# Attention in two half sweeps, then a feed-forward block: scores and exponentials of the first ten steps made one step ahead, in areas of five PSUM banks

## Chip, cores and metric

The kernel runs on one core of a Trainium2 chip. The metric is device time in microseconds of one execution, lower is better. Engines: TensorE (PE) for matmuls, VectorE (DVE), ScalarE (ACT), GpSimd (POOL) and SyncE (SP), which issues most DMAs.

## What is computed

```python
# q, k, v: (8, 8, 576, 64) fp32; tau = 0.02
scores = scale * np.matmul(q, k.transpose(0, 1, 3, 2))       # scale = 1/8
thresh = np.max(scores, axis=-1, keepdims=True) - tau
scores = np.where(scores >= thresh, scores, -1000000000.0)
scores = scores - np.max(scores, axis=-1, keepdims=True)
attn = np.exp(scores)
attn = attn / (np.sum(attn, axis=-1, keepdims=True) + 1e-09)
x = np.matmul(attn, v)              # then (B,H,S,D) -> (B*S, H*D) = (4608, 512)
h = x @ w_in                        # w_in (512, 2048)
g = np.maximum(h, 0.0) ** 2
out = g @ w_out                     # w_out (2048, 512)
```

## The kernel before

Attention runs over "visits". A visit is one pair of heads of one batch; within it a "step" is one block of 128 queries (blocks 0 to 3, and a last block of 64, index 4, which is handled for both heads together). The first batch is done in two sweeps over its four head pairs (`visits`, L813): visits 0 to 3 take query blocks 0 and 1 (steps 0 to 7), visits 4 to 7 take blocks 2, 3 and 4 (steps 8 to 19). In this way the first 256 output rows of all heads are ready after step 10, and the feed-forward work on them (`chunk_at`, L851, pieces placed by `fill`, L929) starts there. Steps before that are called early (`early()`, L863). Later visits take all five blocks in one go. All engines' orders are written out by hand: the loop at L1096 emits instructions, and each engine runs its own in that order.

A step consists of:

- `scores` (L258): per head two matmuls over 288 keys each into PSUM, then `maxima` (L304), one reduce on DVE per head. Scores of a step go to `pairs[0:2]`, banks 0 to 3, of step 1 to banks 4 to 7. The matmul of one head uses the upper 64 rows of the array, of the other the lower 64.
- `exponents` (L319): on ACT a scaled maximum (L322), a threshold (L323) and one exponential per head (L325) from PSUM to one of three slots for weights.
- `threshold` (L328): on DVE, per head, one operation that compares the scores in PSUM with the threshold, multiplies and sums (L337), then a small reduce and a reciprocal. `divide` (L342): on POOL one small and two large operations (L345, L347).
- two steps later `turn` (L378): nine 128x128 transposes on PE in three parts, each part into a bank from `take`, and copied to `wT` by ACT (L387).
- three steps later `mix` (L499): twenty records of value matmuls on PE (L502) into a bank from `take("tx", (4, 5))`, copied to `xT` by ACT (L485).

Around it: `load_qk` (L171) loads queries and keys of a visit, all 576 rows of both, as 32-column pieces, by DMAs that SP issues; `prep` (L232) turns them on DVE (L247) into `qT` (one buffer) and `kT` (two buffers). A piece of the feed-forward weights is rounded in some steps (`pieces`, L935; `round_weights`, L138): two operations on ACT (L149, L150), two on DVE (L152, L154), two on POOL (L156, L158), and a new piece is then loaded (L136, 512 KB). In the early steps that is the first step of visits 1, 2 and 3, and every step from 8 on.

The order of an early step s before, from the loop at L1096: scores of s, parts 0 and 1 of the turn of s-2, exponents of s, values of s-3, part 2 of the turn of s-2, threshold of s, rounding, divide. In the last step of a visit the next visit's queries and keys are turned (`lay`, L1126). The parts of a turn take banks 4, 5 and, for part 1, 6, 7.

`AT` (L113) is a table of four areas of 576 columns that the last part of the kernel uses, two per head, alternating between odd and even blocks; neighbours share a bank:

```python
AT = {(0, 0): (128, 384), (0, 1): (704, 320), (1, 1): (1280, 256), (1, 0): (1856, 192)}
```

The first number is where an area begins in PSUM (512 columns make a bank), the second how many of its columns lie before the next bank.

## Time and profile before

| | us |
|---|---|
| median of three runs | 1335.18 (1333.57 to 1335.2) |
| profiled execution | 1333.83 |
| its span | 1332.0 |
| PE busy in the span | 1295.4 (97%) |
| DVE, ACT, POOL busy | 927.9, 583.0, 786.0 |
| 30 to 60 us: PE, DVE, ACT, POOL busy | 25.65, 24.41, 21.85, 17.59 of 30 |
| 60 to 140 us: PE, DVE, ACT, POOL busy | 73.31, 60.35, 60.04, 68.88 of 80 |

How to read it: busy times are sums over one execution on the core; the ends of matmuls are modelled, so a busy PE is not PE at its peak. A row of a timeline or of a chain has the start in us from the span's start, the length, the engine, the line of the code and how many records were merged (a matmul in fp32 is two records). In brackets stands how long the engine was idle before, and the instruction that ended it.

### The profile page before, as it was taken

The page shows a single profiled execution, that of the slowest core. Times are in us where ns is not written, and L with a number is a line of the kernel's source. Part 1 is how long each engine was busy: PE and PEld are TensorE (multiplying, and loading weights), DVE is VectorE, ACT ScalarE, POOL GpSimd, SP SyncE. Part 2 cuts the span into 40 slices and gives each one's busy share as a digit, 9 for nine tenths or more (in the row PEclk, how much of TensorE's full clock was granted, in tenths as well). Part 3 has the DMA queues.
Part 4 walks back from the last instruction along what each step waited for, and adds up shares of the span by engine and source line. Part 5 has one row for each costly group of instructions (what it writes and reads, how often), then busy time and mean ns, then how long its engine had stood idle before and what let it go on. Part 6 is the DMA issues. An engine that isn't in the chain of part 4 may idle for free.

```text
span 1332.0 us, 25215 instructions
## 1 busy us (share of the span) xinstructions
PE 1295.4 (97%) x9112; PEld 1078.0 (81%) x9112; DVE 927.9 (70%) x2026; ACT 583.0 (44%) x1357; POOL 786.0 (59%) x915
## 2 busy tenths in 40 slices
PE   7898899999999999999999999999999999999998
PEld 5676556888787979797878878888897988889997
DVE  6877776877777878787777776868687877632131
ACT  4776674235262625343534343434443443421321
POOL 4689875775755565474665665747474747454351
PEclk7999999999999999999999999999999999999999
DMA  8764531648786968776766776676686767520000
GB/s 159 160 153 117 144 91 36 159 111 184 166 196 140 214 152 199 167 172 161 167 155 157 163 179 166 168 149 172 148 186 143 178 150 161 161 70 6 12 17 16
DMA packets 330126, 186.69 MB, mean 140 GB/s; under 512 B 291441, under 2 KB 291473, under 8 KB 323601
## 3 DMA queue, kind: packets, MB, share of 16 engines
q1 hardware_dynamic: 317696, 116.87, 46.5%
q0 software_dynamic: 10000, 67.92, 12.8%
q8 instruction: 72, 1.18, 0.4%
q10 hardware_dynamic: 2304, 0.29, 0.2%
q14 instruction: 54, 0.43, 0.1%
HBM read 109.22 MB, written 68.42 MB: 133 GB/s over the span
## 4 chain that ended last, share of the span: by engine, by line
PE 86%; DVE 4%; ACT 3%; POOL 2%; DMA 2%; issue 1%; SPq 0%; ACTq 0%; DVEq 0%; POOLq 0%
PE big L659 29%; PE big L765 28%; PE big L502 10%; PE big L289 8%; PE big L548 3%; PE big L273 3%; PE big L730 2%; PE big L386 2%; DVE st L310 1%; ACT wT L387 1%; DMA wT<-aside 1%; DVE w L337 1%; ACT w L325 1%; DMA aside<-turned 1%; POOL w L347 1%
## 5 line engine op out<-in xcount | busy, mean ns | idle before, releaser
L337 DVE SCALAR_TENSOR_TENSOR w<-big,st,w 128x576 f32<-128x576 f32 x269 | 207.1, 805 | 96.8 <-ACT w L325 96.5
L310 DVE TENSOR_REDUCE st<-big 128x1 f32<-128x576 f32 x288 | 204.2, 748 | 93.8 <-PE big L289 61.7
L347 POOL TENSOR_SCALAR w<-w,st 128x576 f32<-128x576 f32 x269 | 246.6, 926 | 26.4 <-DVE st L340 21.4
L765 PE MATMUL big<-wo,gsum 128*128 128x256 f32 x1088 | 243.8, 382 | 0.0
L765 PEld LDWEIGHTS big<-wo,gsum 128*128 128x128 f32 x1088 | 204.4, 190 | 37.0 <-issue 8.1
L659 PE MATMUL big<-xT,w_in_sb 128*128 128x128 f32 x1536 | 187.4, 277 | 1.3 <-DVE g L671 1.2
L659 PEld LDWEIGHTS big<-xT,w_in_sb 128*128 128x128 f32 x1536 | 178.5, 192 | 10.6 <-issue 8.1
L765 PE MATMUL big<-wo,g 128*128 128x256 f32 x816 | 185.3, 382 | 0.1
L325 ACT ACTIVATE w<-big,st 128x576 f32<-128x576 f32 x269 | 183.8, 734 | 0.0
L765 PEld LDWEIGHTS big<-wo,g 128*128 128x128 f32 x816 | 151.6, 190 | 26.1 <-issue 6.5
L502 PE MATMUL big<-wT,vs 128*64 128x128 f32 (+5 forms) x1700 | 164.2, 355 | 8.3 <-ACT wT L387 4.2
L502 PEld LDWEIGHTS big<-wT,vs 128*64 128x64 f32 (+1 forms) x1700 | 97.1, 137 | 72.0 <-issue 20.7
L322 ACT ACTIVATE st<-st 128x2 f32<-128x2 f32 (+1 forms) x148 | 30.3, 205 | 258.2 <-DVE st L310 257.1
L345 POOL TENSOR_SCALAR st<-st 128x2 f32<-128x2 f32 (+1 forms) x148 | 35.2, 238 | 169.3 <-DVE w L337 163.5
L408 POOL DMA_DIRECT2D aside<-turned x50 | 29.9, 597 | 177.9 <-DVE turned L437 173.7
L671 DVE TENSOR_TENSOR g<-big,g 128x512 f32<-128x512 f32 x96 | 64.7, 676 | 82.4 <-PE big L659 76.8
L289 PE MATMUL big<-kT,qT 64*128 64x256 f32 (+3 forms) x768 | 106.9, 416 | 0.0
L289 PEld LDWEIGHTS big<-kT,qT 64*128 64x128 f32 x768 | 84.5, 186 | 14.5 <-issue 5.0
L667 ACT ACTIVATE g<-g 128x512 f32<-128x512 f32 x96 | 60.2, 628 | 62.9 <-DVE g L671 62.7
L538 POOL TENSOR_TENSOR gsum<-g 128x512 f32<-128x512 f32 x34 | 46.2, 1358 | 69.8 <-ACT g L668 69.6
L668 ACT ACTIVATE g<-g 128x512 f32<-128x512 f32 x128 | 80.7, 630 | 4.1
L431 DVE STREAM_TRANSPOSE turned<-w 128x512 f32<-128x512 f32 x100 | 70.2, 702 | 0.0
(114 smaller groups left out, 2039.0 us busy)
## 6 DMA issues: line engine op xcount, KB each, us to landing
aside<-turned POOLq DMA_DIRECT2D x50, 1152.0 KB, 4.8
wT<-aside SPq DMA_DIRECT2D x200, 288.0 KB, 5.4
vs<-in_v_dram SPq DMA_DIRECT2D x72, 128.0 KB, 6.1
ql<-in_q_dram SPq DMA_DIRECT2D x126, 72.0 KB, 5.0
wo<-in_moe_w_in_dram SPq DMA_DIRECT2D x16, 512.0 KB, 4.6
wo<-in_moe_w_out_dram SPq DMA_DIRECT2D x16, 512.0 KB, 3.8
out_dram<-osb POOLq DMA_DIRECT2D x32, 256.0 KB, 3.6
kl<-in_k_dram SPq DMA_DIRECT2D x113, 72.0 KB, 2.9
```

The source lines that it names most:

```text
L289: nc.tensor.matmul(big[to, at + x0:at + x1], lhsT, keys[u * D:(u + 1) * D, x0:x1], start=True, stop=True)
L310: nc.vector.tensor_reduce(out=mx[:, u:u + 1], in_=sc[u], axis=AX.XY, op=ALU.max)
L325: nc.scalar.activation(out=w[:, u, :].rearrange("p (h k) -> p h k", h=2), in_=sc[u], func=AF.Exp, bias=bias[:, u:u + 1], scale=SCALE)
L337: nc.vector.scalar_tensor_tensor(out=wu, in0=sc[u], scalar=thr[:, u:u + 1], in1=wu, op0=ALU.is_ge, op1=ALU.mult, accum_out=sm[:, u:u + 1])
L347: nc.gpsimd.tensor_scalar(out=w[:, u, :], in0=w[:, u, :], scalar1=z[:, u:u + 1], scalar2=rcp[:, u:u + 1], op0=ALU.add, op1=ALU.mult)
L431: move(wb[:, 0:h, :, :], whole_[:, 0, :, :, :])
L502: nc.tensor.matmul(ps[u * D:(u + 1) * D, :], vs[n % 2][rows, u * (NBLK + 1) + c, :], wT[rows, at // REST:(at + ps.shape[1]) // REST, NBLK ...
L659: nc.tensor.matmul(to[:, f, :], factor(j, p, q, c)[:, f * P:(f + 1) * P], part[:, c, :], start=(p in "125" and f == 0 and c == 0), stop=(p ...
L667: nc.scalar.activation(out=to, in_=to if src is None else src, func=AF.Relu)
L668: nc.scalar.activation(out=to, in_=to, func=AF.Square)
L671: nc.vector.tensor_tensor(out=x, in0=to, in1=x, op=ALU.add)
L765: nc.tensor.matmul(to, left[:, f, :], wo[:, slot, f, :], start=(f == 0), stop=(f == HF - 1))
```

## The change

Seven edits, all in the first 20 steps. First, early steps get a function of their own, `early_step`: scores and exponents of step s+1 are emitted in step s, before the threshold of s. Second, for steps 2 to 9 the scores go to the four areas of `AT`, by turns for odd and even steps, in banks 0 to 4, and each head's matmuls are cut at the bank's edge. Third, turns and values of early steps take their banks from 5, 6, 7, and the three copies of a turn come behind the exponents on ACT. Fourth, in the early steps the next visit's queries and keys are turned in the first step of a visit, not in the last. Fifth, in the two sweeps of the first batch only the queries of the sweep's own blocks are loaded and turned (8 or 10 of 18 blocks of 32 rows), and the keys of the first visit are turned in two halves. Sixth, the weight pieces of visits 1 to 3 are rounded in their second step. Seventh, the small operation on `ntau` goes from DVE to POOL. From step 10 on the instructions follow each other as before, but for the narrower loads and turns of the queries of visits 5 to 7.

```diff
+    def columns(t, n):
+        first = FIRST * P // 32
+        return slice(0, S // 32) if t is k or n >= 2 * HP else slice(0, first) if n < HP else slice(first, S // 32)
...
     def load_qk(n):
         for x, t in ((rows_of(n)[1], k), (rows_of(n)[0], q)):
+            cols = columns(t, n)
             for m in range(4):
...
-                queue.dma_start(out=to[:, last:, :], in_=src[:, 0:S // 32 - last, :])
+                queue.dma_start(out=to[:, cols.start + last:cols.stop, :], in_=src[:, cols.start:cols.stop - last, :])
...
     def prep_part(t, n):
-        nc.vector.transpose(to, rows.rearrange("p c d -> p (c d)"))
+        for x in (slice(0, HALF // 32), slice(HALF // 32, S // 32)) if t is k and n == 0 else (columns(t, n),):
+            nc.vector.transpose(to[:, x.start * 32:x.stop * 32], rows[:, x, :].rearrange("p c d -> p (c d)"))
...
     def scores(s):
-        if i == NBLK:
+        if 1 < s < min(chunk_at):
+            for u in range(n):
+                at, cut = sorted(AT.values())[2 * u + s % 2]
+                rows = slice(u * D, (u + 1) * D)
+                for x0, x1 in ((0, cut), (cut, S)):
+                    nc.tensor.matmul(big[:, at + x0:at + x1], qT[rows, i * P:(i + 1) * P], kT[vis % 2][rows, x0:x1],
+                                     start=True, stop=True)
+                sc[u] = big[:, at:at + S].rearrange("p (h k) -> p h k", h=2)
+        elif i == NBLK:
...
     def turn(vis, i, part):
-        ps = take("mm", (6, 7)) if early() and part == 1 else take("tx", (4, 5))
+        ps = take("tx", (5, 6, 7) if early() else (4, 5))
...
-            nc.scalar.copy(wT[:, 2 * i:2 * i + 2, 3 * part:3 * part + 3, :].rearrange("p g c q -> p c g q"),
-                           ps[:, 0:3, :].rearrange("p c (g q) -> p c g q", g=2))
+            return lambda: nc.scalar.copy(wT[:, 2 * i:2 * i + 2, 3 * part:3 * part + 3, :].rearrange("p g c q -> p c g q"),
+                                          ps[:, 0:3, :].rearrange("p c (g q) -> p c g q", g=2))
...
     def mix(n, cols):
-            ps = take("tx", (4, 5))[:, 0:cols.stop - cols.start]
+            ps = take("tx", (5, 6, 7) if early() else (4, 5))[:, 0:cols.stop - cols.start]
...
-            x = int(n > 0 and i == 0)
+            x = int(n > 0 and i == 1)
...
-    nc.vector.tensor_scalar(out=ntau8, in0=ntau8, scalar1=-1.0 / SCALE, scalar2=None, op0=ALU.mult)
+    nc.gpsimd.tensor_scalar(out=ntau8, in0=ntau8, scalar1=-1.0 / SCALE, scalar2=None, op0=ALU.mult)
...
+    def early_step(s):
+        n, i = steps[s]
+        first = i == visits[n][1][0]
+        now = list(range(sum(pieces[:s]), sum(pieces[:s + 1])))
+        if first and n + 2 < 2 * HP:
+            load_qk(n + 2)
+        if s == 0:
+            scores(0)
+            exponents(*steps[0])
+        if s + 1 < min(chunk_at):
+            scores(s + 1)
+        if first and n < HP:
+            prep(n + 1)
+        if not first:
+            split_left(n)
+        copies = [turn(*steps[s - 2], part) for part in range(3)] if s > 1 else []
+        if s + 1 < min(chunk_at):
+            exponents(*steps[s + 1])
+        for fn in copies:
+            fn()
+        for p in now:
+            round_weights(p, 0)
+        if s in mixes:
+            mix(*mixes[s])
+        threshold(n, i)
+        for p in now:
+            for stage in (1, 2, 3):
+                round_weights(p, stage)
+        divide(n, i)
+        for p in now:
+            end_rounding(p)
+        if first and n:
+            load_v(n)
...
     for s in range(END + 1):
         state["step"] = s
+        if early():
+            rounded_by.append(state["rounded"])
+            done += pieces[s]
+            early_step(s)
+            continue
```

## Prediction

> **What bounds the kernel now.** I read first the page's busy slices, then the chain of work that ended last in the first 100 us, then single instructions of that stretch. The slices: over the span TensorE (PE) is nearly full, except in the first two slices (33 us each). There a saving or a loss moves the end; the change touches only this stretch and the loads of steps 10 to 19.

> ```profile
> PE   7898899999999999999999999999999999999998
> PEclk7999999999999999999999999999999999999999
> ```

> The chain in order of time (start, us, engine and line), here step 8's scores to step 9's:

> ```profile
> 49.19 1.97 PE big L273 x7
> 51.16 0.49 PE big L386 x3
> 51.65 0.02 issue
> 51.67 0.86 ACT wT L387 x2
> 52.53 0.10 ACT st L322
> 52.64 0.05 ACT st L323
> 52.69 0.04 issue
> 52.73 0.75 ACT w L325
> 53.48 0.02 issue
> 53.51 0.84 DVE w L337 x2
> 54.34 0.04 issue
> 54.39 1.97 PE big L273 x7
> ```

> A closed loop: scores, a turn, two copies, the first exponential, the threshold, and then the next scores, which overwrite the banks that the threshold read. It is 5.20 us, and scores stand 5.20 apart at 33.60, 38.80, 43.99, 49.19 and 54.39; steps 2 and 3 took 6.85 and 7.26 (scores at 14.70, 21.55, 28.81). No engine is full in it. The links that the new order needs, from the timeline (start, length, engine, line; in brackets idle time and who ended it):

> ```profile
> 28.81 1.56 PE L273 MATMUL big<-kT,qT 64*128 64x288 f32 x8
> 50.46 1.49 DVE L310 TENSOR_REDUCE st<-big 128x1 f32<-128x576 f32 x2 [0.20 <-PE big L273]
> 57.93 1.37 ACT L325 ACTIVATE w<-big,st 128x576 f32<-128x576 f32 x2
> 59.19 0.49 ACT L242 COPY qmid<-qT 64x64 f32<-64x64 f32 x2
> 65.99 0.86 ACT L387 COPY wT<-big 128x384 f32<-128x384 f32 x2 [0.48 <-PE big L386]
> 66.52 1.31 PE L502 MATMUL big<-wT,vs 128*64 128x128 f32 x20 [0.24 <-ACT wT L387]
> 67.76 0.55 PE L386 MATMUL big<-ident,w 128*128 128x128 f32 x3
> ```

> The reader sees: maxima start 50.46 - 49.19 = 1.27 after their scores start (the wait was for PE) and last 1.49; two exponentials hold ACT for 59.19 - 57.93 = 1.26; the values' matmuls start 66.52 - 65.99 = 0.53 after the copy that they wait for, and hold PE for 67.76 - 66.52 = 1.24.

> [...] the L386 x3 at 67.76 start only as the values end. [...] PE idled 3.82 us before 14.70, the granted clock was 0.50 from 16 to 28, eight score records took 3.02 us there and 1.56 at 28.81.

> **The change part by part.**

> *The new loop.* In steps 2 to 9 the order on PE is: scores of s+1, nine transposes of s-2, values of s-3. On ACT: exponents of s+1, three copies of s-2, rounding, the copy of the values. A step takes four banks out of three (5, 6, 7), so the values of s-3 write the bank that the first copy of s-2 must have read. That is an added wait: the values wait for a copy, which stands behind the exponents of s+1 on ACT, which wait for maxima, which wait for scores. Behind the values on PE stand the scores of s+2, and the maxima wait for them. So one step cannot be shorter than: scores to maxima 1.27; two maxima to ACT's first small operation 1.46 + 0.03 (pipelined, 1.45 to 1.49 in the rows); small operations to first exponential 0.31 (52.42 to 52.73); exponentials 1.26; first copy to values 0.53; values 1.24. Sum 6.10, against 5.20: +0.90 a step. The threshold has left the loop; maxima, the second exponential and the values have entered. I take 6.10; bounds 5.7 (scores of both heads overlap, as the 1.56 hints) and 6.5 (the second exponential also overwrites the slot that the transposes of s-2 read: those end at scores start + 1.6 + 1.4 + 0.2 = 3.2, while it starts at 3.07 + 0.64 = 3.71, so it costs nothing unless they slip by 0.5). Bank waits of the thresholds on the exponents of s+1 end at exponents' start + 3.0; the next scores start at + 3.03: covered, barely.

> *Engines' own floor.* DVE per two steps: four maxima 2.98, four thresholds 3.18 (53.51 to 55.10 is two), small ones 0.56, rounding 0.85, transposes 0.36 + 0.73: 8.67, 4.33 a step. ACT: 2 x (0.31 + 1.26 + 3 x 0.37 + 0.17) + 1.25 = 6.95, 3.5 a step. Neither binds.

> *Start.* Scores 0 stood at 8.57, behind two transposes (7.08 to 8.52) and DVE's ntau. Now q has 8 of 18 blocks, k is turned in halves, ntau goes to POOL (idle then; its DMA landed before, and ACT needs it only after 10): gone, but the twenty warm-up transposes hold PE to 7.76, so scores 0 at 7.8, -0.8. Scores 2 then at 13.9 (same 6.13 behind), cold clock, 3.02; maxima end 17.7, first exponential to 18.7; scores 3 (whose parts share banks with those of step 2, so wait for its exponentials) 18.7 to 21.9; nine transposes at half clock 2.2 (17.66 to 19.84), to 24.1; the threshold of step 2 starts behind the exponential of step 3, scores 4 at about 24.9, against 28.81. But step 3 then still runs at half clock: 6.10, + 0.96 for one head's scores, + about 0.4 of the values: scores 5 at 32.4 against 33.60, -1.2. Bounds -2.2 (clock back at 25) and +0.5 (back after 33).

> *Steps 5 to 8:* four intervals, 4 x 0.90 = +3.6.

> *The hand-over.* Step 10 keeps the old order, so its scores are not made ahead: from scores 9, the values of step 5 end at 6.10, transposes of step 7 to 7.5; ACT finishes three copies (5.5), rounding 1.25 (6.75), the values' copy and qmid (7.2), then the copy that the values of step 6 wait for: 7.73, + 1.24 = 8.97, scores 10. Before, 59.73 - 54.39 = 5.34: +3.6.

> *Smaller edits, at nothing.* q's smaller loads are as many DMAs, and SP's issue is 0.49 each for 8 KB or 72 KB; no engine waited for a DMA from 28 to 60. They save DMA packets only. Narrower transposes save 0.4 of DVE a visit, beside DVE's wait for the exponential (0.2 to 1.1 a step). The transposes move one step earlier, past a threshold: q of visit 3, issued by 26.1, landed 2.7 later and was read at 36.28, so 7.5 of slack less a 6.1 step remains 1.4; if that cover fails, 1 us once. A weight piece (ACT 1.25, DVE 0.85, POOL 2.5, one 512 KB DMA on SP) goes from first to second steps; five are done by step 9 both ways, and POOL's 4.4 in such a step lies within 6.1. From step 10 the programs agree, so the delay is carried: PE is busy 73.3 of 80 us from 60 to 140 and 1176 of 1192 after.

> Sum: -1.2 + 3.6 + 3.6 = +6.0. The profiled execution took 1333.83 (span 1332.0, 1.83 around it): 1339.8. The median of the runs shown is 1335.18, 1.35 above that execution; on it 1341.2, said as 1341.0.

> **The rivals.**

> *Faster, 0.07.* The values' wait for the first copy costs less than I think (the copy ends before PE gets there), and DVE becomes the bound at 4.33 to 4.6. The profile's idle DVE speaks for it, the closed chain of waits against. It decides where the step falls below about 4.9, since 5 steps and 2.7 of hand-over behind 32.4 must then reach scores 10 before 59.73. At 4.5 the loop gives 32.4 + 22.5 + 2.7 = 57.6, -2.1, and with a good start and a shorter hand-over -4: 1331.

> *No difference, 0.13.* Step 5.4: 5 x 0.7 less and the better start (-2.2): +1.5, 1336.7. For it: concurrent heads in the scores, start of step 4 four us earlier. Against: the maxima are DVE's 1.46 whatever PE does.

> *Clock stays low, 0.12.* PE would be busy about 4.0 of 6.1 us (before: 4.0 of 5.2), with a gap of 1.5. If the clock drops or comes back late, each cold step adds 0.96 + 1.1; three to four such steps give 7 on top of the 6.0: 1348. Against: such a step is 80% busy, which restored the clock at 28.

> **The numbers.** Forecast 0.68 at 1341.0, its own range 1338 to 1345. Range for all: 1336.5 (no difference) to 1347 (late clock). This kernel's measurement tells about 0.2%, 2.7 us, from no change. Faster 0.07, same 0.13, slower 0.80.

> **What would show it.** Right: the first values row of each step waits for a copy of ACT; scores 6.1 apart from step 5; maxima wait for scores; about 9 us from scores 9 to 10; DVE and ACT idle more from 30 to 60. Wrong: spacing under 5, DVE without idle time, the clock at 0.5 past 33, or a delay at step 10 that has shrunk by 140 us.

## The result, and the profile after

The change made the kernel slower: 1343.84 us (median of 4 runs, 1341.88 to 1344.95) against 1334.46 (4 runs), a ratio of 1.0069, 95% interval 1.0056 to 1.0082. The profiled execution has a span of 1341.1 us against 1332.0, so +9.1; 6.0 had been worked out. By the medians it is +9.4.

The busy slices of the page after the change. The first two are lower than before (33.5 us each); of the rest only the fifth differs, 9 for 8:

```profile
PE   6698999999999999999999999999999999999998
PEclk7899999999999999999999999999999999999999
```

PE is less busy in both (6 and 6 tenths, before 7 and 8), and its clock is lower in the second (8 tenths, before 9). What the slices can't show is where. The start of each step's scores on PE's timeline does:

| scores of step | 0 | 2 | 3 | 4 | 5 | 6 | 7 | 8 | 9 | 10 | 11 |
|---|---|---|---|---|---|---|---|---|---|---|---|
| before | 8.57 | 14.70 | 21.55 | 28.81 | 33.60 | 38.80 | 43.99 | 49.19 | 54.39 | 59.73 | 64.23 |
| after | 7.69 | 14.06 | 18.13 | 24.07 | 31.74 | 38.27 | 45.40 | 51.92 | 59.05 | 68.53 | 73.68 |

The changed program leads by 4.7 us at step 4 and by 1.9 at step 5, is 4.7 behind at step 9, 8.8 at step 10 and 9.5 at step 11. A scores group that stood at 210.36 before stands at 219.90: the delay is carried to the end.

The chain of the changed kernel in order of time (start, length, engine, tile and line), for the step that answers to the one shown of before:

```profile
37.03 1.31 PE big L517 x20
38.34 1.18 PE big L276 x6
...
39.54 1.44 DVE st L325 x2
...
41.00 0.03 ACT st L337
...
41.29 1.35 ACT w L340 x2
42.64 0.38 ACT wT L402
...
43.07 2.40 PE big L517 x20
45.47 1.65 PE big L276 x6
```

This is the loop that the prediction drew: values (L517), scores, two maxima, the small operations, two exponentials, the first copy, and the values again. The threshold has gone from it. From 37.03 to 43.07 it took 6.04. But the next values are the same twenty records, and take 2.40 instead of 1.31: they run at half clock.

PE's timeline after (in brackets: idle time, and who ended it):

```profile
43.07 2.40 PE L517 MATMUL big<-wT,vs 128*64 128x128 f32 x20 [2.42 <-ACT wT L402]
...
50.68 1.31 PE L517 MATMUL big<-wT,vs 128*64 128x128 f32 x20 [2.43 <-ACT wT L402]
...
56.72 2.40 PE L517 MATMUL big<-wT,vs 128*64 128x128 f32 x20 [2.42 <-ACT wT L402]
```

From 37.03 on every step's values wait for the copy, with PE idle 2.42 to 2.43 us, and every second step is then cold (its values run at half clock). The values' starts lie 6.04 and 7.61 apart by turns, 13.65 for two.

Stretches of the changed kernel show when the clock falls (columns: stretch, its length, busy us of PE, PEld, DVE, ACT and POOL, granted clock, DMA share, GB/s):

```profile
36.18:39.59 3.41, 2.56 (x29) 2.12 (x30) 1.76 (x7) 1.82 (x5) 1.90 (x4) 1.00 0.43 73
39.59:43.01 3.42, 1.06 (x9) 0.82 (x8) 1.71 (x3) 2.01 (x6) 0.20 (x1) 1.00 0.30 68
43.01:46.42 3.41, 3.35 (x25) 3.02 (x27) 2.30 (x8) 2.17 (x6) 0.85 (x1) 0.50 0.12 17
46.42:49.83 3.41, 1.83 (x14) 1.24 (x12) 2.67 (x5) 1.22 (x4) 3.24 (x5) 1.00 1.02 225
```

The stretches are laid so that the clock is the same within each: in the first 100 us of this trace it changes only at borders that lie 3.41 us or a multiple of it apart (low from 15.70 to 22.53, 25.94 to 32.77, 43.01 to 46.42 and 56.66 to 60.08). In the one ahead of the fall at 43.01 PE was busy 1.06 of 3.42 us (31%). The stretch at 0.50, busy 3.35 of 3.41, is followed by 1.00 again; the stretch with 1.83 (54%) is followed by one more at 1.00. The busy share is not all that counts, as the parts on half of the array's rows and on the clock below show. In the trace of before the clock was low from 14.77 to 28.42, which is 13.65, or four times 3.41. In the changed kernel's trace two steps last 13.65 us, as long as the four stretches above (36.18 to 49.83), so the same step of each pair meets the emptiest stretch, and the falls at 43.01 and 56.66 lie 13.65 apart.

### The profile page after: what moved, and what is told of

Read it like the earlier page. It is cut to its first block, busy times and chain, and to the rows that moved or that the text cites. A ratio compares the mean times of both kernels' runs of the same rounds, so it can differ in the third digit from the quotient of the medians.

```text
span 1341.1 us, 25225 instructions
## 1 busy us (share of the span) xinstructions
PE 1294.9 (97%) x9112; PEld 1078.6 (80%) x9112; DVE 928.6 (69%) x2026; ACT 583.4 (44%) x1357; POOL 787.8 (59%) x916
## 3 DMA queue, kind: packets, MB, share of 16 engines
q8 instruction: 72, 1.18, 0.4%
## 4 chain that ended last, share of the span: by engine, by line
PE 86%; DVE 4%; ACT 3%; POOL 3%; DMA 2%; issue 1%; SPq 0%; DVEq 0%; POOLq 0%; ACTq 0%
PE big L674 28%; PE big L780 28%; PE big L517 11%; PE big L304 8%; PE big L563 3%; PE big L745 2%; PE big L288 2%; DVE st L325 2%; PE big L401 2%; ACT w L340 1%; PE big L276 1%; DMA wT<-aside 1%; DVE w L352 1%; ACT wT L402 1%; POOL w L362 1%
## 5 line engine op out<-in xcount | busy, mean ns | idle before, releaser
L325 DVE TENSOR_REDUCE st<-big 128x1 f32<-128x576 f32 x288 | 204.2, 748 | 102.0 <-PE big L304 60.6
L517 PE MATMUL big<-wT,vs 128*64 128x128 f32 (+5 forms) x1700 | 166.0, 358 | 21.2 <-ACT wT L402 17.2
L780 PEld LDWEIGHTS big<-wo,g 128*128 128x128 f32 x816 | 151.6, 190 | 26.1 <-issue 6.5
L517 PEld LDWEIGHTS big<-wT,vs 128*64 128x64 f32 (+1 forms) x1700 | 98.7, 139 | 85.2 <-ACT wT L402 22.1
L337 ACT ACTIVATE st<-st 128x2 f32<-128x2 f32 (+1 forms) x148 | 30.2, 204 | 279.7 <-DVE st L325 278.7
```

The lines of the kernel that those rows point to most:

```text
L325: nc.vector.tensor_reduce(out=mx[:, u:u + 1], in_=sc[u], axis=AX.XY, op=ALU.max)
L517: nc.tensor.matmul(ps[u * D:(u + 1) * D, :], vs[n % 2][rows, u * (NBLK + 1) + c, :], wT[rows, at // REST:(at + ps.shape[1]) // REST, NBLK ...
L780: nc.tensor.matmul(to, left[:, f, :], wo[:, slot, f, :], start=(f == 0), stop=(f == HF - 1))
```

## The experiments

Each ratio is to runs of the kernel before that were made on the same chip together with the kernel compared (medians 1333.53, 1333.69 and 1333.53; for the changed kernel it was 1334.46). A loss is therefore given against those runs of before. Where a kernel has one added line above, its line numbers are one higher than the changed kernel's.

**The first copy ahead of the exponents.** It takes the values' wait out of the loop with the order alone.

```diff
         copies = [turn(*steps[s - 2], part) for part in range(3)] if s > 1 else []
+        for fn in copies[:1]:
+            fn()
         if s + 1 < min(chunk_at):
             exponents(*steps[s + 1])
-        for fn in copies:
+        for fn in copies[1:]:
             fn()
```

> The changed kernel, with the first of the three copies of a turn put ahead of the exponents of s+1 on ACT, so that the values no longer wait behind the exponents; nothing else moves. Loop theory (values wait for that copy, and scores of s+2 stand behind the values on PE): the wait goes, the next limit is DVE and the banks shared with the exponents, steps 5.4 to 5.5 us apart where the changed kernel has 6.0 at full clock and 6.8 on average; four intervals give 5 to 6 us, and the hand-over at step 10 stays at about 9: 1337.5 to 1339.5. Clock theory alone (the loop is 6.0 anyway and only the low clock costs): scores stay 6.0 or more apart, 1340 or more. Order theory (what costs is that DVE has the maxima of s+1 ahead of the threshold of s): no change, 1343 to 1344.

Measured 1335.95 (21 runs), ratio 1.0017 (1.0010 to 1.0023): moving one copy takes the loss from 9.4 to 2.4 us. The time lies below the range of the loop theory: the steps are shorter than it had them (5.29 for 5.4 to 5.5), the hand-over is longer, and the runs of before made with it are 0.9 lower. The two other theories had 1340 or more, and fell. Scores from step 5 on stand at 30.45, 35.60, 41.03, 46.19 and 51.62, 5.29 apart on the mean. PE's timeline of this kernel:

```profile
38.64 1.31 PE L517 MATMUL big<-wT,vs 128*64 128x128 f32 x20
41.03 1.97 PE L276 MATMUL big<-kT,qT 64*128 64x320 f32 x8 [1.08 <-DVE w L352]
```

The values no longer wait, and the wait that is left is that of the scores for a threshold: that of two steps back, since odd and even steps take the areas by turns and these scores overwrite the area that it read. The clock stays at 1.00 from 30 to 59. Of the 7.05 us won at scores 10 (61.48 against 68.53), 1.29 are there at scores 5, 6.14 are won from there to scores 9, and 0.38 are lost in the hand-over, 9.86 here: PE waits there for POOL and ACT, one stretch (56.42 to 59.83) is 52% busy, and the clock falls at 59.83.

**Something for PE to do in the gap.** It leaves the loop as it is and fills part of PE's wait with six 128x128 matmuls of `ident`, whose output nobody reads.

```diff
+    FILL = 6
...
         copies = [turn(*steps[s - 2], part) for part in range(3)] if s > 1 else []
+        if copies and s + 1 < min(chunk_at):
+            free = bank[(5, 6, 7)[used["tx"] % 3]][:, 3 * P:4 * P]
+            for _ in range(FILL):
+                nc.tensor.matmul(free, ident, ident, start=True, stop=True)
```

> The changed kernel with six more matmuls of 128 columns (1.3 us) behind the transposes of each of steps 2 to 8, into unused columns, in the 2.4 us in which PE waits for the copy. Clock theory (the gap lets the clock fall in every second step, which then takes 1.6 us more): clock 1.00 from 30 to 60, steps 6.0 to 6.1 apart, four intervals give 3, the hand-over 0.5: 1340 to 1341. If the clock's falls have nothing to do with the gap: 0.5 stays in every second step, time as in the changed kernel or up to 1 more. If the low clock did not cost anything: clock 1.00, time unchanged.

Measured 1338.44 (5 runs), ratio 1.0036 (1.0023 to 1.0048): more work for PE, and the loss falls from 9.4 to 4.9 us. Its timeline, and then its stretch from 30 to 60 us:

```profile
39.05 1.50 PE L1133 MATMUL big<-ident 128*128 128x128 f32 x12
41.63 1.31 PE L518 MATMUL big<-wT,vs 128*64 128x128 f32 x20 [1.08 <-ACT wT L403]
```

```profile
30.00:60.00 30.00, 24.62 (x245) 21.18 (x243) 21.32 (x51) 18.17 (x47) 16.05 (x21) 1.00 0.52 112
```

The clock is 1.00 throughout (0.84 without the filling), and scores from step 5 on (30.79, 36.83, 42.87, 48.91, 54.95) are 6.04 apart each time. From step 5 on this is the loop by itself, with no clock in it; what stays of the loss, 4.9 us, is the loop and the hand-over (8.99), less the earlier start. It came out lower than expected, in part because the clock was up in step 4 too (scores 5 at 30.79), in part because the runs of before made with it are 0.9 lower.

**Three instead of six** (`FILL = 3`).

> The run with the filling matmuls, but three in place of six, so that a gap of about 1.8 us stays on PE in each of steps 2 to 8 (2.4 without, 1.1 with six). [...] somewhere between, 1.00 throughout (steps 6.04, 1338 to 1339.5) or still falling in some steps (6.4, 1341).

Measured 1337.61 (one run, so without an interval), clock 1.00 from 30 to 60, 6.04 apart: 0.83 us a step of filling was enough in it.

**One.**

> As the changed kernel, with one added full matmul a step (0.28 us) in TensorE's gap; its output is read by nobody. The emptiest stretch of 3.41 us is then about 38% busy (31% without, 49% with three). Both theories of the clock (a share of busy time near half, or of the array) say that the clock still falls in some steps: 1341 to 1344 us, scores about 6.8 apart on the mean. Rival, only the length of the gap counts and 2.4 us is just over the edge: at a gap of 2.15 the clock stays up, 6.04 apart, 1338.

Measured 1344.72 (4 runs), ratio 1.0077 (1.0060 to 1.0094), a little above the expected range; clock 0.80 from 30 to 60, with every second one of the later steps cold. The stretches ahead of the falls in the loop (at 38.38, 52.03 and 65.69) are 40 to 46% busy. One filler doesn't help at a gap of 2.19 to 2.20 us, so the rival with an edge just under 2.4 us fell.

**Three that use half of the array's rows.**

```diff
-                nc.tensor.matmul(free, ident, ident, start=True, stop=True)
+                nc.tensor.matmul(free, ident[0:D], ident[0:D], start=True, stop=True)
```

> As the changed kernel, with three added fp32 matmuls a step in TensorE's gap, this time over 64 of the array's 128 rows; they last as long as the three full ones did (0.83 us a step), and their output is read by nobody. Theory A, the clock follows the share of TensorE's busy time in stretches of 3.41 us: the emptiest stretch is 49% busy, as with three full ones, so the clock stays at 1.00 from 30 to 60, scores 6.04 apart, 1337 to 1339 us. Theory B, what counts is the share of the array that works, so that a matmul over half of the rows counts half: (0.93 + 0.42 + 0.07)/3.41, about 41%, so the clock falls to 0.50 in some steps, spacing 6.8 there, and the time is 1341 to 1344.

Measured 1340.81 (4 runs), ratio 1.0051 (1.0036 to 1.0066), between the two expectations. The four executions fall apart: two with a mean clock of 0.996 took 1338.97 and 1339.84, two with 0.989 and 0.992 took 1341.97 and 1341.77. In the profiled one (clock 0.992) the clock fell twice, at 48.76 and at 62.41; scores 8 are late by 0.8. Its stretches around the first fall:

```profile
45.35:48.76 3.41, 1.86 (x19) 1.50 (x19) 3.40 (x7) 2.38 (x7) 3.24 (x5) 1.00 0.85 207
48.76:52.17 3.41, 3.41 (x27) 2.90 (x22) 0.55 (x4) 0.66 (x3) 2.51 (x4) 0.50 0.28 47
```

and one of the three emptiest stretches in the loop of the kernel with three full fillers (1.66 to 1.68 us busy):

```profile
37.92:41.34 3.42, 1.68 (x17) 1.49 (x17) 1.71 (x3) 2.14 (x6) 0.33 (x1) 1.00 0.45 98
41.34:44.75 3.41, 3.41 (x38) 2.88 (x39) 3.14 (x10) 1.94 (x5) 0.98 (x1) 1.00 0.14 29
```

A stretch 54% busy with half-row fillers was followed by half clock; one 49% busy with full ones was not. So PE's busy time alone doesn't decide, and neither does the length of the gap: PE waited 1.55 us for the copy ahead of that fall, and 1.74 with the three full fillers. A share of the array that works does fit these two, but it was tried in one form only. The changed kernel's own trace, at its start, has a still busier stretch that was followed by half clock:

```profile
22.53:25.94 3.41, 2.26 (x12) 1.30 (x10) 2.90 (x8) 2.39 (x5) 0.78 (x2) 1.00 0.45 71
25.94:29.35 3.41, 2.21 (x10) 1.78 (x9) 1.22 (x3) 2.23 (x6) 1.08 (x2) 0.50 0.44 96
```

It was 66% busy, but 1.87 of its 2.26 us are scores, each of whose matmuls takes 64 rows; in the stretch with 1.83 us above, which left the clock up, they are 0.70. This points the same way. The exact measure and its edge stay open.

**The narrower loads alone** (the kernel before, with `columns`, the first keys in two halves, and `ntau` on POOL).

> The kernel before with only the narrower loads and turns of queries, the first keys turned in halves and the small ntau operation on POOL. Prediction's view (loads and turns are hidden): scores 0 at 7.7 in place of 8.57, and at most 0.8 us of it reach the end: 1333.5 to 1334.5. Rival (the loads are a good part of the earlier start of the changed kernel, 24.1 against 28.8 for scores 4): 2 to 4 us less, 1330.5 to 1332.5.

Measured 1332.14 (21 runs), ratio 0.9988 (0.9981 to 0.9994). Scores 0 at 7.57, scores 5 at 32.18 (before 33.60), and then 5.20 apart as before: a gain of 1.4 us, all from the start. As a gain it lies between the two expectations (at most 0.8, and 2 to 4); the time lies in the rival's range only because the runs of before made with it are 0.9 lower. The rest of the change thus costs 1341.1 - 1330.3 = 10.8 us of span, not 9.1.

**The changed kernel with full loads.**

```diff
-        return slice(0, S // 32) if t is k or n >= 2 * HP else slice(0, first) if n < HP else slice(first, S // 32)
+        return slice(0, S // 32)
```

> The changed kernel with all 576 query rows loaded and turned again in both sweeps. Prediction's view: loads are hidden, start 0.3 to 1 later, 1344 to 1345. Rival (the narrower loads carry the earlier start, their loss delays the turns that now stand one step earlier): 2 to 4 more, 1346 to 1348.

Measured 1344.33 (4 runs), ratio 1.0080 (1.0066 to 1.0094). Its scores come 0.9 us later at step 5 (32.63) and 0.3 to 0.4 later at steps 6 to 11 (38.67 to 73.98), and its interval overlaps that of the changed kernel. The 0.5 that is won back from step 5 to 6 is the clock's: here it is up from 29.60, so that interval takes 6.04, where the changed kernel, with its clock low to 32.77, took 6.53. The rival's 2 to 4 us fell. Whether the new order hides the loads altogether is not shown: against its own runs of before this kernel loses 10.8 us, the changed one 9.4, and the intervals are too wide to part the two.

**The divide ahead of the rounding on POOL**, with the six fillers, for the 0.65 us that steps 10 to 11 lose (below).

```diff
         threshold(n, i)
+        divide(n, i)
         for p in now:
             for stage in (1, 2, 3):
                 round_weights(p, stage)
-        divide(n, i)
```

> The run with the six filling matmuls, with the divide of a step ahead of its rounding on POOL in the early steps. Theory on the hand-over (the turn of step 8 in step 10 waits for a divide that stands behind a late rounding on POOL): scores of steps 10 and 11 stand 4.5 apart in place of 5.15, time 0.5 to 0.7 below that run, 1337.8. Rival (the wait moves to ACT's rounding, which is late as well): 5.1 stays, 1338.4.

Measured 1338.79 (5 runs), ratio 1.0037 (1.0024 to 1.0051), the same as without. Scores 10 to 11 still take 5.25. The turn no longer waits for a divide, but the scores of step 11 then wait 0.97 for a threshold, behind ACT's copies and roundings, which end up late as well. Besides, the scores of steps 6 and 8 came some 0.26 later each (6.30 after the scores before them, in place of 6.04). The theory fell; POOL is not the only one that is late there.

**The rounding at the start of the step, and two copies ahead.** Two edits at once on the first experiment's order; the lines are shown against the changed kernel.

```diff
+        for p in now:
+            round_weights(p, 0)
         if s + 1 < min(chunk_at):
             scores(s + 1)
+        for p in now:
+            for stage in (1, 2):
+                round_weights(p, stage)
...
+        for fn in copies[:2]:
+            fn()
         if s + 1 < min(chunk_at):
             exponents(*steps[s + 1])
-        for fn in copies:
+        for fn in copies[2:]:
             fn()
-        for p in now:
-            round_weights(p, 0)
...
         for p in now:
-            for stage in (1, 2, 3):
-                round_weights(p, stage)
+            round_weights(p, 3)
```

> The run with a copy ahead of the exponents, now with two copies ahead, and with the rounding of a weight piece at the start of its step on ACT and ahead of the threshold on DVE. Theory on what bounds that run (DVE, in steps with a piece: maxima, exponential, two thresholds, small ones, rounding): odd steps lose 0.3 to 0.85, steps 4.9 to 5.2 apart in place of 5.29, 1334 to 1336. Rival (PE or the banks shared with the exponents bound it): 5.3 stays or more, 1336 to 1337.

Measured 1338.51 (one run): steps of 5.19 and 5.83 by turns, and stretches at half clock from 25.8 to 32.6 and from 56.5 to 59.9. The theory fell; the steps (5.51 on the mean) fit the rival's 5.3 or more, the time lies above both ranges. With two edits the run doesn't tell which of them lengthened the step. What bounds the first experiment at 5.29 is shown only as far as its wait.

**The old order, with the copies late and four banks.** It makes nothing ahead. From the change it takes the narrower loads and the idea that copies stand behind the exponents, and gives turns and values banks 4 to 7 in the early steps. Left out here are the lines of the narrower loads, the values' banks, and the lines that let a copy be issued later than its transposes.

```diff
-        ps = take("mm", (6, 7)) if early() and part == 1 else take("tx", (4, 5))
+        ps = take("tx", (4, 5, 6, 7) if early() else (4, 5))
...
-            turn(*old, 0)
-            turn(*old, 1)
+            copies = [turn(*old, 0), turn(*old, 1)]
+            if not (early()):
+                copies.pop(0)()
+                copies.pop(0)()
         if on:
             exponents(n, i)
...
+        if old:
+            for fn in copies:
+                fn()
```

> The kernel before with the narrower loads, and in the early steps two of the three copies of a turn put behind the exponents on ACT, with four banks (4 to 7) in turn for transposes and values, so that neither values nor scores wait for a copy that stands behind the exponents. No scores or exponents are made ahead. Loop theory: the old loop loses the copies and what is before them and keeps scores to maxima 1.27, two maxima 1.46, small operations 0.31, first exponential 0.75, threshold 0.84: 4.65, or DVE's own work, 4.7 to 5.0 on average, in place of 5.20; five intervals give 1 to 2.5 below the narrower loads alone: 1329.5 to 1331. Rival (it was the making ahead that a shorter step needs): 5.2 stays, 1332.

Measured 1328.75 (5 runs), ratio 0.9958 (0.9944 to 0.9972): 4.9 us faster than the kernel before, where the narrower loads alone won 1.4. It is also below what was expected: of the 3.3 us of span that it wins over the narrower loads, 1.5 are there at scores 5 (30.65 against 32.18), and four steps of 0.46 make 1.8. Its chain in order of time:

```profile
44.87 1.25 PE big L280 x5
...
46.15 1.50 DVE st L317 x2
...
47.67 0.21 ACT st L329
...
48.06 0.65 ACT w L332
...
48.73 0.84 DVE w L344 x2
```

The step is scores, maxima, small operations, one exponential and one threshold, 4.74 apart (44.87, 49.62). No copy is in it, and PE is 26.43 of 30 us busy from 30 to 60. The late copies and the fourth bank were not run apart.

## Why the prediction was right, and where it was short

Slower was forecast, at 1341.0 within 1338 to 1345, and 1343.84 came. The times below are of PE's timelines, as differences to before; the last column is the kernel with six fillers, where the clock keeps out from step 4 on.

| term | predicted | after | with fillers |
|---|---|---|---|
| scores 5 (33.60 before) | -1.2 | -1.86 | -2.81 |
| four steps, scores 5 to 9 (20.79 before) | +3.6 | +6.52 | +3.37 |
| hand-over, scores 9 to 10 (5.34 before) | +3.6 | +4.14 | +3.65 |
| scores 10 to 11 (4.50 before) | 0 | +0.65 | +0.65 |
| the rest of the span | 0 | -0.3 | +0.3 |
| sum, the span | +6.0 | +9.1 | +5.2 |

**The added wait and its loop: right.** 6.10 was predicted, 6.04 measured, and moving one copy out of the loop took the loss from 9.4 to 2.4 us. Two of its terms were off and cancel: the two exponentials hold ACT for 1.35 in place of 1.26 (41.29 to 42.64 in the chain), and the values start 0.43 in place of 0.53 behind their copy. With the clock out of the way the sum of 6.0 stands against 5.2; that they lie so close is in part luck, since a start better by 1.6 makes up for 0.95 behind scores 10 that was put at nothing.

**The hand-over: right as far as the trace tells.** No run changed it alone.

```profile
66.76 1.24 ACT L402 COPY wT<-big 128x384 f32<-128x384 f32 x3
...
67.29 1.31 PE L517 MATMUL big<-wT,vs 128*64 128x128 f32 x20 [0.34 <-ACT wT L402]
```

Behind scores 9 (59.05) the values that wait for that copy start after 8.24 us, where 7.73 was predicted, and scores 10 after 9.48, for 8.97; 0.49 of it is the clock (below).

**The clock: the step that failed.** The prediction put "Clock stays low" among its rivals at 0.12, and set against it: "such a step is 80% busy, which restored the clock at 28". Neither half holds. Its own 4.0 of 6.1 us are 66%; near 80% was the step of before, 4.0 of 5.2. In the changed kernel a warm step is 60% busy: values 1.24, scores 1.18 and transposes 1.20, 3.62 of 6.04. The scores are shorter than the 1.97 of before, since both heads' banks are free at once and their matmuls run together (the first of one head starts at 38.27, of the other at 38.28); before, the second head waits for its own threshold, which starts 0.74 behind the first head's (53.51 and 54.25), and the group is stretched from 1.24 to 1.97. The gap was written as 1.5, where the prediction's own numbers left 6.1 - 4.0 = 2.1, and 2.4 came. And the stretch ahead of the rise at 28.42 was busy throughout (3.41 of 3.41), not 80%; an equally full one earlier in the trace of before was followed by 0.50:

```profile
14.77:18.18 3.41, 3.41 (x11) 2.36 (x12) 3.13 (x11) 1.25 (x2) 2.20 (x5) 0.50 1.05 357
...
25.01:28.42 3.41, 3.41 (x26) 2.75 (x25) 2.59 (x6) 2.53 (x6) 2.67 (x3) 0.50 0.79 132
```

After the first, mostly scores over 64 rows (2.96 of 3.41 us), the clock stayed at 0.50 for three more stretches; after the second, transposes and values over all 128 rows, it was 1.00. So in this trace a full stretch doesn't tell by itself that the clock comes back.

So the rival came true in part, and on top of the forecast, not in its place. A cold step costs +1.09 for the values (2.33 before the next scores instead of 1.24) and +0.49 from scores to maxima (1.76 instead of 1.27), 1.58 together, where the rival had 0.96 + 1.1. Two of the four steps from 5 to 9 are cold: 3.16 us, less 4 x 0.06 by which the warm loop is shorter than predicted, are the 2.92 by which that term was missed. The hand-over's 9.48 against 8.97 has one cold 0.49 in it. That 1343.84 still lies below 1345 owes something to luck: no part of that bound was worked out from a clock that falls while the loop runs, and a start better by 0.7 and runs of before with a median 0.7 lower (1334.46 for 1335.18) took off part of what the clock added.

**The start: right in kind.** Scores 0, 2, 3 and 4 at 7.69, 14.06, 18.13 and 24.07 (7.8, 13.9, 18.7 and 24.9 predicted). Ahead of scores 3 PE waited 1.90 us for an exponential of step 2, whose areas share banks with theirs. Scores 5 came 0.7 sooner than predicted. The clock was up from 22.5 to 26 and low again to 32.8; with the fillers it is up from 23.9 on, and scores 5 come another 0.95 sooner.

**Edits at nothing: nearly.** The loads alone are worth 1.4 us in the old order; the prediction counted 0.8 of it, at scores 0, and the remainder goes with the clock (no run parts the two), which is back at 24.5 instead of 28.4 (scores 4 at 26.98 instead of 28.81). The moved turns of queries and keys and the moved rounding were not run apart; from 28 to 60 no wait of PE is put down to them. Not foreseen: the 0.65 from scores 10 to 11. The turn of step 8, in step 10, waits there for POOL's divide, and the scores of step 11 for a threshold, in PE's timeline after:

```profile
70.83 0.44 PE L401 MATMUL big<-ident,w 128*128 128x128 f32 x2 [0.32 <-POOL w L362]
...
73.68 1.24 PE L288 MATMUL big<-kT,qT 64*128 64x288 f32 x8 [0.70 <-DVE wo L352]
```

POOL had waited 3.3 us for ACT before the rounding that stands ahead of that divide. It is there with the fillers too, so it isn't the clock; putting the divide first only moved the wait to ACT and DVE. That ACT's order in the hand-over is the cause was not shown.

**The other rivals fell.** "Faster" and "no difference" wanted steps below 4.9 or of 5.4; none was below 6.0. DVE and ACT, busy 24.41 and 21.85 us from 30 to 60 before, are busy 18.48 and 15.99 after: no engine's floor was near. The delay was carried, as said: +9.54 at 210.

## What to carry to other kernels

When work is made ahead, write down each engine's queue as it then stands and follow the wait that a smaller set of buffers adds: here one copy, queued behind two exponentials that wait for a product of the next step, closed a loop around three engines. Then work out the idle time of TensorE that the new loop leaves, stretch by stretch and not as a mean (here a warm step was 60% busy, the stretch ahead of the fall 31%), before trusting the durations of a warm trace. What helped was to take the copies out of the loop and give turns and values a fourth bank, two edits in one run, without any scores made ahead.
